# Delta rule and expert router: chunks of 32 tokens for four sequences at once, in place of chunks of 64 for two

## The chip, the cores and the metric

The kernel runs on one core of a Trainium2 chip. A core has TensorE (matrix products, results into PSUM), VectorE, ScalarE and GpSimd for everything else, SyncE as the queue that issues most DMA transfers, and 16 DMA engines behind it. PSUM has eight banks of 512 fp32 values in each of its 128 partitions. The metric is the device time of one execution in microseconds (us). Before the change it is 802.09 us, the median of three runs (800.87 to 803.17). The profile is of one execution of its own, whose span is 794.5 us.

## The reference: what is computed

Two blocks, one after the other. The first is attention by the delta rule, for 4 sequences (B) of 8 heads, 768 tokens and head size 48. Each head carries a 48x48 state from token to token:

```python
k_n = k / (np.linalg.norm(k, axis=-1, keepdims=True) + 1e-06)
for t in range(S):
    kt, vt, bt = (k_n[:, :, t], v[:, :, t], beta[:, :, t, None])
    y[:, :, t] = np.einsum('bhd,bhde->bhe', q[:, :, t], state)
    v_old = np.einsum('bhde,bhd->bhe', state, kt)
    state = state + bt[:, :, :, None] * np.einsum('bhd,bhe->bhde', kt, vt - v_old)
```

The second takes the 3072 tokens of 384 values each, finds for every token the best of 8 experts by cosine similarity, and runs the token through that expert alone:

```python
logits = xn @ en.T / tau
expert_idx = np.argmax(logits, axis=1)
...
h = np.maximum(x[mask] @ w1[e], 0.0)          # 384 -> 1024
out[mask] = gate_w[mask, None] * (h @ w2[e])  # 1024 -> 384
```

Token after token the recurrence would have 768 steps. The kernel takes it in chunks: inside a chunk the tokens depend on one another through a triangular matrix that is made of products of k with k. Its inverse is built, the chunk's values are multiplied by it ("solve"), and only then is the state brought forward, once for the chunk.

## The kernel before

A unit of work is one chunk of 64 tokens, 8 heads, and two of the four sequences, one in partitions 0 to 63 and one in 64 to 127. There are 12 chunks and two units for each, 24 units. The two units of a chunk do not depend on one another, and each depends on the unit of the same sequences one chunk earlier.

The inverse is built only of the two diagonal 32x32 blocks of each 64x64 matrix, by doubling: blocks of 2, 4, 8, 16 and 32. Each of the four levels has two steps on TensorE, `level` and `grow`. All of these steps use one helper, which issues 16 matmuls on the 64x64 tiles of the array at upper left and lower right:

```python
def apply(lhsT, rhs, times=1):
    n = rhs.shape[2]
    p = bank([128, times, H, n])
    for h in range(H):
        for i in range(2):
            mm(p[HALF[i], :, h], lhsT[HALF[i], h], rhs[HALF[i], h].unsqueeze(1).broadcast_to([C, times, n]))
    return p if times > 1 else p[:, 0]

def level(U, s):
    p = apply(U["G32"], U["T"], 2)
    yield
    U["P"] = PP[s][U["n"] % 2]
    nc.vector.copy_predicated(...)          # P <- where the mask of this level says so, p

def grow(U):
    p = apply(U["P"], U["W"], 2)[:, 0]
    yield
    U["W"] = wk.tile([128, H, BL], F32, name="W", ...)
    act_copy(U["W"], p)
    yield
    transposed_blocks(U, p)                 # T, by VectorE, out of the same bank
```

A `yield` ends a part: the parts of many units are issued in turn. In the names of the profile, `bank<-T,G` is a level's step, `bank<-W,P` a grow's, `bank<-R,WL` a solve with the inverse, `bank<-Z,G` a product with a part of the gram, `bank<-S_bd,KT` the products of k and q with the state, and `pair<-Z,KK` the update of the state.

As the inverse is known for blocks of 32 only and the chunk has 64 tokens, the chunk is solved in three steps: the first block, its influence on the second, and the whole:

```python
def of_states(U):
    V, c = U["R"], U["c"]
    if c > 0:
        p = [of_state(U, a) for a in range(2)]       # k and q times the state, a bank each
        yield
    U["R"] = narrow("R", 3)
    if c > 0:
        nc.vector.tensor_tensor(U["R"], p[0], V, op=ALU.subtract)
        yield
        U["Yq"] = narrow("Yq", 3)
        act_copy(U["Yq"], p[1])
    ...

def solve1(U):
    p = apply(U["W"], U["R"])
    yield
    U["Z1"] = narrow("Z1")
    act_copy(U["Z1"], p, K["first"])

def solve2(U):
    p = apply(U["G"][:, 0].rearrange("p j jj c -> p (j jj) c"), U["Z1"])
    yield
    nc.vector.scalar_tensor_tensor(out=U["R"], in0=p, scalar=K["second"], in1=U["R"], op0=ALU.mult, op1=ALU.add)

def solve3(U):
    p = apply(U["W"], U["R"])
    yield
    U["Z"] = narrow("Z", 3)
    act_copy(U["Z"], p)

def state(U):
    ...
    p = pair([NP, D])
    for j in range(NP):
        for i in range(2):
            for jj in range(2):
                mm(p[HALF[jj], i, j], U["K"][HALF[i], 2 * j + jj], U["Z"][HALF[i], 2 * j + jj])
    yield
    S_ = S_u[U["u"]]
    nc.vector.tensor_tensor(S_, p.rearrange("p i j d -> p j i d"), S_, op=ALU.add)
    yield
    nc.gpsimd.tensor_tensor(S_bd[U["u"]]..., S_..., K["own"]..., op=ALU.mult)   # each head on its own block
```

`first` and `second` are columns of ones and zeros that keep one half of each 64 partitions. `state` and `gram` write into a pair of banks and use all four 64x64 tiles of the array; `outputs` is one more `apply`, with the masked product of k and q.

PSUM is divided for good into four single banks and two pairs. The order in which parts are issued comes out of a small model in the kernel's own Python code, with a length for each part, that runs while the program is built. Loads are issued by SyncE, two transfers (one for a sequence) for each of k, q and v of a unit:

```python
def load(U, dst, src):
    t0 = U["c"] * C
    for i in range(2):
        nc.sync.dma_start(out=dst[i * C:(i + 1) * C],
                          in_=src[2 * U["u"] + i, :, t0:t0 + C, :].rearrange("h p d -> p h d"))
```

k and q of the first unit are loaded once ahead of everything and then once more by the unit's own `load`, whose copy is the one used. When a group of four units is through, its tokens are routed: logits, the best expert, a place in that expert's list, and the rows of x go to memory. After all groups, the second part gathers 128 tokens of one expert at a time.

Of the kernel before, what the change touches and what calls it, by code (L numbers as in the profile page):

```python
# [16 lines left out]
C = 64  # L17
BL = 32
T = 128
LEVELS = (2, 4, 8, 16)  # L20
# [3 lines left out]
def kernel(  # L24
# [35 lines left out]

    nc = tc.nc
    B, H, S, D = q.shape
    NC, NP, Dm, N = S // C, H // 2, H * D, B * S
    NU = B // 2
# [21 lines left out]

    def bank(shape):
        return ps.tile(shape, F32, name="bank", tag="bank", bufs=4)

    def pair(shape):  # L90

        t = ps.tile([128, 2, 512], F32, name="pair", tag="pair", bufs=2)
        n = 1
        for d in shape:
            n *= d
        t = t[:, :, 0:n]
        if len(shape) == 2:
            return t.rearrange("p r (a b) -> p r a b", a=shape[0])
        return t.rearrange("p r (a b c) -> p r a b c", a=shape[0], b=shape[1])
# [7 lines left out]
    hc = [128, H, C]  # L107
    jc = [128, NP, 2, C]

# [5 lines left out]
    def clear(t):  # L115
        nc.gpsimd.memset(t[:, :, D:C], 0.0)

    def load(U, dst, src):

        t0 = U["c"] * C  # L120
        for i in range(2):
            nc.sync.dma_start(out=dst[i * C:(i + 1) * C],  # L122
                              in_=src[2 * U["u"] + i, :, t0:t0 + C, :].rearrange("h p d -> p h d"))
# [11 lines left out]
    UNITS = [dict(n=n, c=n // NU, u=n % NU) for n in range(NC * NU)]  # L135
# [3 lines left out]
    bt = ac.tile([NU * H, NC, 2, C], F32, name="bt")  # L139
    for u in range(NU):  # L140
        for i in range(2):
            (nc.sync if u else nc.scalar).dma_start(out=bt[u * H:(u + 1) * H, :, i],
                                                    in_=beta[2 * u + i].rearrange("h (c t) -> h c t", t=C))
# [4 lines left out]
    half = cpool.tile([128, NU, H], F32, name="half")  # L148
    nc.vector.memset(half, 0.5)
    root = ac.tile([128, 1], F32, name="root")  # L150
    nc.scalar.activation(root, half[:, 0, 0:1], ACT.Sqrt)


    prow = ac.tile([128, C], I32, name="prow")
    nc.gpsimd.iota(prow, pattern=[[0, C]], base=0, channel_multiplier=1)
    xor_i = ac.tile([128, C], I32, name="xor_i")
    nc.gpsimd.iota(xor_i, pattern=[[1, C]], base=0, channel_multiplier=0)
    clear(KK[0])
    clear(QQ[0])
    trow = ac.tile([128, C], I32, name="trow")  # L160
    nc.vector.tensor_single_scalar(trow, prow, C - 1, op=ALU.bitwise_and)
    col_f = ac.tile([128, C], F32, name="col_f")
    nc.vector.tensor_copy(col_f, xor_i)
    nc.vector.tensor_tensor(xor_i, xor_i, trow, op=ALU.bitwise_xor)
    xor_f = ac.tile([128, C], F32, name="xor_f")
    nc.vector.tensor_copy(xor_f, xor_i)
    trow_f = ac.tile([128, C], F32, name="trow_f")
# [3 lines left out]
    id64 = ac.tile([128, 1, C], F32, name="id64")  # L171
    nc.vector.tensor_single_scalar(id64[:, 0, :], xor_f, 0.0, op=ALU.is_equal)
    id32 = ac.tile([128, 1, BL], F32, name="id32")
    nc.vector.tensor_tensor(id32[:, 0], id64[:, 0, 0:BL], id64[:, 0, BL:C], op=ALU.add)
    upper = ac.tile([128, 1, C], F32, name="upper")
    nc.vector.tensor_tensor(upper[:, 0, :], col_f, trow_f, op=ALU.is_gt)
    lower = ac.tile([128, 1, C], F32, name="lower")

    def mask(name, tri, lo, hi):
        m = ac.tile([128, 1, C], F32, name=name)  # L180
        nc.vector.scalar_tensor_tensor(out=m, in0=xor_f.unsqueeze(1), scalar=float(lo), in1=tri,
                                       op0=ALU.is_ge, op1=ALU.mult)
        nc.vector.scalar_tensor_tensor(out=m, in0=xor_f.unsqueeze(1), scalar=float(hi), in1=m,
                                       op0=ALU.is_lt, op1=ALU.mult)
        return m.bitcast(I32)
# [5 lines left out]
    W2 = [ac.tile([128, H, BL], F32, name=f"W2_{i}") for i in range(2)]  # L191
# [6 lines left out]
    betaT, sqb, quot = (ac.tile([128, NC, NU * H], F32, name=name) for name in ("betaT", "sqb", "quot"))  # L198
# [10 lines left out]
    def root_of(U):  # L209
        return sqb[:, U["c"], U["u"] * H:(U["u"] + 1) * H]  # L210

    def beta_by_token():
        psB = bank([128, NC, NU * H])
        for c in range(NC):
            nc.tensor.transpose(psB[:, c], bt[:, c].rearrange("p i t -> p (i t)"), ident[0:NU * H, 0:NU * H])
        nc.vector.tensor_copy(betaT, psB)
# [4 lines left out]
    def more_masks():  # L221
        for name, value in (("second", ALU.is_ge), ("first", ALU.is_lt)):

            K[name] = ac.tile([128, 1], F32, name=name)
            nc.vector.tensor_single_scalar(K[name], trow_f[:, 0:1], float(BL), op=value)
# [5 lines left out]
        for t in S_u:  # L231
            nc.vector.memset(t, 0.0)

    def all_masks():
        for lv in LEVELS[1:]:
            below[lv] = mask(f"below{lv}", lower, lv, 2 * lv)
        for t in XC:
            nc.gpsimd.memset(t[:, :, :, Dm:], 0.0)

        own = K["own"] = ac.tile([128, 1, 2, 1], F32, name="own")  # L240
        nc.vector.tensor_single_scalar(own[:, 0, 1], prow_p, float(C), op=ALU.is_ge)
        nc.vector.tensor_single_scalar(own[:, 0, 0], prow_p, float(C), op=ALU.is_lt)

    prow_p = ac.tile([128, 1], F32, name="prow_p")
    nc.vector.tensor_copy(prow_p, prow[:, 0:1])
    XC = [ac.tile([128, 2, NU, ROW], F32, name=f"XC{i}") for i in range(2)]
    S_u = [ac.tile([128, NP, 2, D], F32, name=f"S{u}") for u in range(NU)]
    S_bd = [ac.tile([128, NP, 2, 2, D], F32, name=f"S_bd{u}") for u in range(NU)]
# [25 lines left out]
    def late_constants3():  # L274

        prow_f = ac.tile([128, 1], F32, name="prow_f")
        nc.vector.tensor_copy(prow_f, prow[:, 0:1])
        nc.vector.tensor_single_scalar(prow_f, prow_f, float(C), op=ALU.is_ge)
        nc.vector.scalar_tensor_tensor(out=prow_f, in0=prow_f, scalar=float(S), in1=trow_f[:, 0:1],
                                       op0=ALU.mult, op1=ALU.add)  # L280
        tok_i = ac.tile([128, NC, NU], I32, name="tok_i")
        nc.gpsimd.iota(tok_i, pattern=[[C, NC], [2 * S, NU]], base=0, channel_multiplier=0)
        tok_f = ac.tile([128, NC, NU], F32, name="tok_f")
        nc.vector.tensor_copy(tok_f, tok_i)
        nc.vector.tensor_scalar(tok_f, tok_f, prow_f, None, op0=ALU.add)
        K["tokid"] = ac.tile([128, NC, NU, ID], I32, name="tokid")
        nc.vector.tensor_copy(K["tokid"], tok_f.unsqueeze(3).broadcast_to([128, NC, NU, ID]))
# [27 lines left out]
    def embeddings1():  # L315
        nc.scalar.activation(esq, emb, ACT.Square, accum_out=ess)
        nc.gpsimd.tensor_tensor(out=ess, in0=ess, in1=half[0:E, 0, 0:1], op=ALU.pow)
# [13 lines left out]
    HALF = (slice(0, C), slice(C, 2 * C))  # L331
# [11 lines left out]
    def prep2(U):  # L343
# [3 lines left out]
        nc.gpsimd.tensor_tensor(out=U["rn"], in0=U["rn"], in1=half[:, 0], op=ALU.pow)  # L347
# [15 lines left out]
    def transposes(U):  # L363
        U["KT"] = wk.tile([128, NP, 2, 128], F32, name="KT", tag="KT", bufs=4)
# [6 lines left out]
        for a in range(2):  # L371
            yield
            act_copy(U["KT"][:, :, a], ps_[a])
# [4 lines left out]
    def gram(U):  # L378

        KT = U["KT"]  # L380
        U["psG"] = p = pair([NP, 2, C])
        for j in range(NP):
            for jj in range(2):
                pr = slice(jj * C, jj * C + D)
                for i in range(2):
                    mm(p[HALF[i], jj, j], KT[pr, j, 0, HALF[i]], KT[pr, j, :, HALF[i]])
        yield
        U["G32"] = wk.tile(hc, F32, name="G32", tag="G32", bufs=3)
        for b, name in enumerate(("first", "second")):
            cols = slice(b * BL, (b + 1) * BL)  # L390
            act_copy(by_head(U["G32"])[:, :, :, cols].rearrange("p j jj c -> p jj j c"), p[:, :, :, 0, cols], K[name])
        yield
        U["W"] = W2[U["n"] % 2]
        for b in range(2):
            cols = slice(b * BL, (b + 1) * BL)
            nc.vector.copy_predicated(by_head(U["W"]).rearrange("p j jj c -> p jj j c"),  # L396
                                      up2[:, :, cols].unsqueeze(1).broadcast_to([128, 2, NP, BL]), p[:, :, :, 0, cols])
# [3 lines left out]
    def gram2(U):  # L401
        p = U["psG"]
        U["G"] = G = wk.tile([128, 2, NP, 2, C], F32, name="G", tag="G", bufs=5)
        for a in range(2):
            act_copy(G[:, a].rearrange("p j jj c -> p jj j c"), p[:, :, :, a])
            yield
        M = U["M"] = G[:, 1].rearrange("p j jj c -> p (j jj) c")
        nc.gpsimd.tensor_tensor(M, M, upper.broadcast_to(hc), op=ALU.mult)

    def transposed_blocks(U, src):  # L410
        U["T"] = wk.tile([128, H, BL], F32, name="T", tag=f"T{U['n'] % 3}", bufs=1)
        nc.vector.transpose(U["T"].rearrange("p h c -> p (h c)"), src.rearrange("p h c -> p (h c)"))  # L412

    def apply(lhsT, rhs, times=1):
# [5 lines left out]
        for h in range(H):  # L420
            for i in range(2):
                mm(p[HALF[i], :, h], lhsT[HALF[i], h], rhs[HALF[i], h].unsqueeze(1).broadcast_to([C, times, n]))
        return p if times > 1 else p[:, 0]

    def level(U, s):
# [4 lines left out]
                                  below[s].rearrange("p o (b c) -> p o b c", b=2).broadcast_to([128, H, 2, BL]),  # L430
                                  p.rearrange("p b h c -> p h b c"))

    def grow(U):
        p = apply(U["P"], U["W"], 2)[:, 0]
        yield
        U["W"] = wk.tile([128, H, BL], F32, name="W", tag=f"W{U['n'] % 3}", bufs=1)
# [4 lines left out]
    def grow_last(U):  # L441
# [3 lines left out]
        for b, name in enumerate(("first", "second")):  # L445
            act_copy(U["W"][:, :, b * BL:(b + 1) * BL], p, K[name])
# [4 lines left out]
    def of_state(U, a):  # L451

        p = bank([128, H, D])
        for j in range(NP):
            for i in range(2):
                mm(p[HALF[i], 2 * j:2 * j + 2], U["KT"][:, j, a, HALF[i]], S_bd[U["u"]][:, j, i])
        return p

    def of_states(U):

        V, c = U["R"], U["c"]
        if c > 0:
            p = [of_state(U, a) for a in range(2)]
            yield
        U["R"] = narrow("R", 3)
        if c > 0:
            nc.vector.tensor_tensor(U["R"], p[0], V, op=ALU.subtract)
            yield
            U["Yq"] = narrow("Yq", 3)
            act_copy(U["Yq"], p[1])  # L470
        else:
            nc.vector.tensor_scalar_mul(U["R"], V, -1.0)

    def solve1(U):
        p = apply(U["W"], U["R"])
        yield
        U["Z1"] = narrow("Z1")
        act_copy(U["Z1"], p, K["first"])

    def solve2(U):  # L480
# [529 lines left out]
```

## Time and profile before

| | from 0 to about 462 us: attention | from 474 us to the end: experts |
|---|---|---|
| what runs | 24 units, 7 groups of routing | 28 tiles of 128 tokens |
| TensorE busy, 160 to 220 us and 480 to 600 us | 59.6 of 60 us | 120.0 of 120 us |
| VectorE busy, same stretches | 34.7 of 60 us | 12.9 of 120 us |
| ScalarE busy | 25.8 of 60 us | 13.1 of 120 us |
| GpSimd busy | 26.2 of 60 us | 23.1 of 120 us |
| share of the DMA engines' time | 0.20 | 0.98 |

Between the two, TensorE stands for 12.6 us until the first gathered tokens arrive.

How such a page is read. A row of the groups has the source line, the engine, the operation, what is written and read by the program's names, the shape and the count; then after the first bar the busy time of the group and the mean of one instruction, and after the second the idle time of that engine just before them with what ended most of it. In order of time, a line has the start, the length, the engine, the line, the operation and the count of a run of like instructions. Matmuls overlap one another: a matmul's own length is far more than its share of TensorE's time, which is the distance from start to start. The line of 40 slices gives the busy share of each fortieth of the span in tenths. Most matmuls stem from one helper line (L334), so they are told apart by their tiles. One matmul statement in fp32 shows as two records.

### The profile page before, as it was taken

The numbers are of one execution on the slowest core, as the hardware profiler recorded it, in microseconds if no ns is written. First come the engines' busy times: TensorE is split into PE (matmuls) and PEld (weight loads), VectorE is DVE, ScalarE is ACT, GpSimd is POOL, SyncE is SP. The second block draws the span as 40 slices with busy tenths as digits, with TensorE's granted clock in tenths as the row PEclk, the third lists the DMA queues.
The fourth block names the chain that finished last, engine by engine and source line by source line (L and its number), as shares of the span: only waits on it lengthen the run. The fifth ranks groups of instructions, "written<-read, shape, count | busy, mean of one in ns | idle before, by whom it ended". The sixth has DMA issues, their size and how long they took to land.

```text
span 794.5 us, 30513 instructions
## 1 busy us (share of the span) xinstructions
PE 725.1 (91%) x13770; PEld 651.1 (82%) x13770; DVE 284.2 (36%) x696; ACT 219.9 (28%) x485; POOL 254.3 (32%) x277
## 2 busy tenths in 40 slices
PE   2889899899989989998998829999999999999993
PEld 2789899799989989998998828877788877788872
DVE  5756546366454636654553330011011011011010
ACT  2544343535344433434352201110111010111010
POOL 4843333365164435525423121221122221122220
PEclk9999999999999999999999759999999999999997
DMA  6653421313132231202001129999999999999996
GB/s 120 121 142 85 130 43 24 86 24 63 20 75 44 39 85 25 44 4 56 5 3 42 28 63 390 390 366 326 343 318 320 330 317 331 347 311 333 318 317 240
DMA packets 137446, 132.46 MB, mean 167 GB/s; under 512 B 86266, under 2 KB 121505, under 8 KB 137314
## 3 DMA queue, kind: packets, MB, share of 16 engines
q1 hardware_dynamic: 132562, 119.15, 48.6%
q0 software_dynamic: 4544, 11.27, 3.8%
q8 instruction: 110, 1.80, 0.9%
q14 instruction: 22, 0.18, 0.1%
q10 hardware_dynamic: 208, 0.05, 0.0%
HBM read 118.78 MB, written 12.45 MB: 165 GB/s over the span
## 4 chain that ended last, share of the span: by engine, by line
PE 61%; DMA 17%; issue 10%; DVE 6%; POOL 2%; ACT 1%; SPq 1%; another core or an unknown queue 0%; POOLq 0%; ACTq 0%; DVEq 0%
PE bank L334 37%; DMA out_dram<-y,ids 14%; PE acc L895 8%; PE acc L902 8%; PE pair L334 3%; PE bank L369 2%; DMA ids<-idmap 1%; PE bank L530 1%; DVE T L412 1%; DVE W L396 1%; DVE P L429 1%; DMA k_in<-in_k_dram 1%; DVE rn L352 1%; PE acc L886 1%; SPq L122 1%
## 5 line engine op out<-in xcount | busy, mean ns | idle before, releaser
L334 PE MATMUL bank<-T,G 64*64 64x64 f32 x3072 | 110.8, 224 | 7.1 <-issue 3.2
L334 PEld LDWEIGHTS bank<-T,G 64*64 64x64 f32 x3072 | 102.1, 139 | 11.1 <-issue 5.0
L897 ACT ACTIVATE hT<-acc 128x512 f32<-128x512 f32 x56 | 33.5, 597 | 280.4 <-PE acc L895 272.8
L334 PE MATMUL bank<-W,P 64*64 64x64 f32 x3072 | 105.5, 220 | 5.1 <-DVE P L429 3.7
L334 PEld LDWEIGHTS bank<-W,P 64*64 64x64 f32 x3072 | 98.1, 136 | 6.4 <-issue 3.6
L895 PEld LDWEIGHTS acc<-xTm,w 128*128 128x128 f32 x864 | 99.3, 192 | 4.8
L905 POOL DMA_INDIRECT out_dram<-y,ids x28 | 28.5, 1017 | 229.2 <-DVE y L904 212.1
L895 PE MATMUL acc<-xTm,w 128*128 128x128 f32 x864 | 99.4, 275 | 0.0
L902 PE MATMUL acc<-w,hT 128*128 128x384 f32 x288 | 95.9, 486 | 0.0
L429 DVE COPY_PREDICATED P<-below,bank 128x512 f32<-128x512 int32 x96 | 69.8, 731 | 44.4 <-PE bank L334 39.2
L902 PEld LDWEIGHTS acc<-w,hT 128*128 128x128 f32 x288 | 53.3, 190 | 33.4
L887 DVE COPY xTm<-acc 128x384 f32<-128x384 f32 x29 | 16.2, 558 | 152.4 <-PE acc L886 152.4
L334 PE MATMUL bank<-R,WL 64*64 64x48 f32 x1536 | 58.4, 221 | 9.5 <-issue 9.5
L503 POOL TENSOR_TENSOR S_bd<-S,own 128x768 f32<-128x768 f32 x22 | 32.3, 1466 | 99.4 <-DVE S L501 99.4
L904 DVE TENSOR_SCALAR y<-acc,xg 128x384 f32<-128x384 f32 x28 | 17.3, 618 | 128.9 <-PE acc L902 128.9
L334 PEld LDWEIGHTS bank<-R,WL 64*64 64x64 f32 x1536 | 53.3, 138 | 11.7 <-issue 11.7
L895 PEld LDWEIGHTS acc<-xTm,w_first 128*128 128x128 f32 x480 | 57.3, 198 | 3.5 <-DVE xTm L887 1.1
L895 PE MATMUL acc<-xTm,w_first 128*128 128x128 f32 x480 | 57.5, 282 | 0.7 <-DVE xTm L887 0.7
L334 PE MATMUL bank<-Z,G 64*64 64x48 f32 x1536 | 55.1, 220 | 2.3 <-issue 1.8
L334 PEld LDWEIGHTS bank<-Z,G 64*64 64x64 f32 x1536 | 51.4, 138 | 2.7 <-issue 1.9
L902 PE MATMUL acc<-w_first,hT 128*128 128x384 f32 x160 | 53.3, 486 | 0.0
L347 POOL TENSOR_TENSOR rn<-rn,half 128x8 f32<-128x8 f32 x24 | 39.5, 1647 | 34.2 <-DVE rn L345 31.7
(167 smaller groups left out, 901.3 us busy)
## 6 DMA issues: line engine op xcount, KB each, us to landing
w<-in_moe_w_dram SPq DMA_DIRECT2D x40, 1536.0 KB
w_first<-in_moe_w_dram SPq DMA_DIRECT2D x20, 1536.0 KB
k_in<-in_k_dram SPq DMA_DIRECT2D x50, 96.0 KB
QQ<-in_q_dram SPq DMA_DIRECT2D x50, 96.0 KB
x_dram<-XC SPq DMA_DIRECT2D x24, 200.0 KB
v_in<-in_v_dram SPq DMA_DIRECT2D x48, 96.0 KB
idmap<-none SPq DMA_DIRECT2D x1, 1792.0 KB
w_first<-in_moe_w_dram SPq DMA_DIRECT2D x8, 192.0 KB
```

The lines of the kernel that those rows point to most:

```text
L122: nc.sync.dma_start(out=dst[i * C:(i + 1) * C], in_=src[2 * U["u"] + i, :, t0:t0 + C, :].rearrange("h p d -> p h d"))
L334: nc.tensor.matmul(out_, lhsT=lhsT, rhs=rhs, start=start, stop=True, skip_group_check=True)
L347: nc.gpsimd.tensor_tensor(out=U["rn"], in0=U["rn"], in1=half[:, 0], op=ALU.pow)
L369: nc.tensor.transpose(p[:, j], src[:, 2 * j:2 * j + 2, :].rearrange("p h d -> p (h d)"), ident)
L429: nc.vector.copy_predicated(U["P"].rearrange("p h (b c) -> p h b c", b=2), below[s].rearrange("p o (b c) -> p o b c", b=2).broadcast_to([1 ...
L503: nc.gpsimd.tensor_tensor(S_bd[U["u"]].rearrange("p j i jj d -> p (j i) jj d"), S_.rearrange("p j i d -> p (j i) d").unsqueeze(2).broadcas ...
L887: nc.vector.tensor_copy(t.xT, psX)
L895: nc.tensor.matmul(psH[:, i, :], lhsT=t.w1[:, j, (f + i) * 128:(f + i + 1) * 128], rhs=t.xT[:, j, :], start=(j == 0), stop=(j == KC - 1))
L897: nc.scalar.activation(t.hT[:, f:f + 4, :], psH, ACT.Relu)
L902: nc.tensor.matmul(psO, lhsT=t.hT[:, f, :], rhs=t.w2[:, f, :], start=(f == 0), stop=(f == NF - 1))
L904: nc.vector.tensor_scalar_mul(y, psO, t.x[:, Dm:Dm + 1])
L905: nc.gpsimd.indirect_dma_start(out=out[:, :], out_offset=bass.IndirectOffsetOnAxis(ap=t.ids[:, 0:1], axis=0), in_=y, in_offset=None, bound ...
```

## The change

The chunk becomes as long as the blocks of the inverse. A unit is now 32 tokens of all four sequences: two sequences share each half of the partitions, 32 partitions each. There are 24 chunks and one unit for each, so again 24 units of the same size, but each unit depends on the one just before it. Since the inverse covers the whole chunk, it is applied directly, in one step in place of three. The state of two sequences has to be told apart inside one half: the right side of the state's update is widened to two copies of Z, each with the other sequence's tokens set to zero, and the products with the state are computed for both and cleared by `first` and `second`. The state is now kept in its block form only, so GpSimd's spreading goes away.

PSUM's eight banks are kept in one list. A part takes one or two of them and hands each back as soon as its last reader is issued. The order of all parts is written down in a table, a number for each part and each unit, and the parts are sorted by it.

The diff, cut to its core:

```diff
-C = 64
-BL = 32
+C = 32
+PC = 2 * C
...
     def bank(shape):
-        return ps.tile(shape, F32, name="bank", tag="bank", bufs=4)
+        b = free.pop(0)
+        taken.append([b])
+        t = psum[b // 2][:, b % 2, 0:512]
...
     def load(U, dst, src):
-        t0 = U["c"] * C
-        for i in range(2):
+        t0 = U["n"] * C
+        for i in range(B):
...
     def transposes(U):
-        U["KT"] = wk.tile([128, NP, 2, 128], F32, name="KT", tag="KT", bufs=4)
+        U["KT"] = wk.tile([128, NP, 2, 4, C], F32, name="KT", tag="KT", bufs=4)
+        U["kT"] = wk.tile([128, NP, 2, PC], F32, name="kT", tag="kT")
...
+            if p is ps_[0]:
+                yield
+                act_copy(U["kT"].rearrange("d j p c -> d j (p c)"), p)
...
+            ps_ = [bank([128, H, D]) for o in range(2)]
+            for j in range(NP):
+                for o in range(2):
+                    for i in range(2):
+                        mm(ps_[o][HALF[i], 2 * j:2 * j + 2], U["KT"][:, j, i, 2 * o:2 * o + 2], S_bd[:, i, j, o])
...
+        nc.vector.scalar_tensor_tensor(out=U["R"], in0=ps_[1], scalar=K["second"], in1=V, op0=ALU.mult,
+                                       op1=ALU.subtract)
+        nc.vector.scalar_tensor_tensor(out=U["R"], in0=ps_[0], scalar=K["first"], in1=U["R"], op0=ALU.mult,
+                                       op1=ALU.add)
+        yield
+        parts = [narrow("Yq1"), narrow("Yq2")]
+        act_copy(parts[0], ps_[0], K["second"])
+        act_copy(parts[1], ps_[1], K["first"])
+        yield
+        U["Yq"] = narrow("Yq", 3)
+        nc.gpsimd.tensor_tensor(U["Yq"], parts[0], parts[1], op=ALU.add)
+
+    def solve(U):
         p = apply(U["W"], U["R"])
         yield
-        U["Z1"] = narrow("Z1")
-        act_copy(U["Z1"], p, K["first"])
-
-    def solve2(U):
-        p = apply(U["G"][:, 0].rearrange("p j jj c -> p (j jj) c"), U["Z1"])
-        yield
-        nc.vector.scalar_tensor_tensor(out=U["R"], in0=p, scalar=K["second"], in1=U["R"], op0=ALU.mult, op1=ALU.add)
-
-    def solve3(U):
-        p = apply(U["W"], U["R"])
+        U["Zx"] = wk.tile([128, H, 2, D], F32, name="Zx", tag="Zx")
+        act_copy(U["Zx"][:, :, 0], p, K["first"])
+        yield
+        nc.vector.tensor_scalar(U["Zx"][:, :, 1], p, K["second"], None, op0=ALU.mult)
         yield
         U["Z"] = narrow("Z", 3)
         act_copy(U["Z"], p)
...
-                    mm(p[HALF[jj], i, j], U["K"][HALF[i], 2 * j + jj], U["Z"][HALF[i], 2 * j + jj])
+                    mm(p[HALF[jj], i, 2 * j:2 * j + 2], U["K"][HALF[i], 2 * j + jj], U["Zx"][HALF[i], 2 * j + jj])
         yield
-        S_ = S_u[U["u"]]
-        nc.vector.tensor_tensor(S_, p.rearrange("p i j d -> p j i d"), S_, op=ALU.add)
-        yield
-        nc.gpsimd.tensor_tensor(S_bd[U["u"]]...
+        for jj in range(2):
+            own = S_bd[HALF[jj], :, :, :, jj].rearrange("p i j o d -> p i (j o) d")
+            nc.vector.tensor_tensor(own, p[HALF[jj]], own, op=ALU.add)
...
+    KEYS = {
+        "load": (-11464,), "prep1": (-8895,), "prep2": (-7076, -7075), "prep3": (-5816, -5815), "scale_v": (-5757,),
+        "transposes": (-3773, -3772, -3771, -3770), "gram": (-2683, -2682, -2681, -2680), "gram2": (92, 93, 3874),
...
+        "of_states": (7169, 7170, 7171, 7172), "solve": (8244, 8245, 8246, 8247), "state": (9397, 9398),
...
+    BASE = (-6100, -2180, 1870, 5807, 9591, 13404, 17210, 20989, 24801, 28644, 32590, 36251, 40157, 44051, 47913,
+            51716, 55405, 59261, 62974, 66795, 70813, 74479, 78270, 82247)
...
+    parts = [(BASE[U["n"]] + key, i, U["n"], name, part) for i, (U, name, part, key) in enumerate(
+        (U, name, part, key) for U in UNITS for name in KEYS for part, key in enumerate(KEYS[name]))]
```

## What was predicted

> **What bounds the kernel now.** I read the page first (busy shares, the 40 slices, the costliest groups), then the engines' busy time in chosen stretches, then TensorE in order of time inside one steady stretch, then the issue queue of SyncE at the start.
>
> ```profile
> PE 725.1 (91%) x13770; PEld 651.1 (82%) x13770; DVE 284.2 (36%) x696; ACT 219.9 (28%) x485; POOL 254.3 (32%) x277
> ...
> PE   2889899899989989998998829999999999999993
> ...
> DVE  5756546366454636654553330011011011011010
> ...
> L334 PE MATMUL bank<-R,WL 64*64 64x48 f32 x1536 | 58.4, 221 | 9.5 <-issue 9.5
> ...
> L334 PE MATMUL bank<-Z,G 64*64 64x48 f32 x1536 | 55.1, 220 | 2.3 <-issue 1.8
> ```
>
> The dip in slices 23 and 24 divides the program: about 462 us of attention, a gap, then from 474 us the expert stage, which the change leaves alone. In both TensorE is at eight or nine tenths; VectorE, its nearest follower, is at half in attention. One matmul statement leaves two records: 16 statements x 24 units x 2 stages give 768, and the row of R,WL shows 1536. That row is solve1 and solve3, the row of Z,G is solve2 and the outputs. A record's mean of 220 ns is no cost: matmuls overlap. The cost is from start to next start, which TensorE in order of time gives:
>
> ```profile
> 186.35 1.10 PE L334 MATMUL pair<-KT 48*64 48x128 f32 x32
> ...
> 303.28 1.11 PE L334 MATMUL bank<-R,WL 64*64 64x48 f32 x32
> 304.20 1.98 PE L334 MATMUL bank<-T,G 64*64 64x64 f32 x61
> 305.97 0.26 PE L334 MATMUL pair<-Z,KK 64*64 64x48 f32 x2
> 306.00 0.28 PE L334 MATMUL bank<-T,G 64*64 64x64 f32 x3
> 306.07 0.66 PE L334 MATMUL pair<-Z,KK 64*64 64x48 f32 x30
> 306.54 1.14 PE L334 MATMUL bank<-W,P 64*64 64x64 f32 x32
> 307.48 1.11 PE L334 MATMUL bank<-Z,G 64*64 64x48 f32 x32
> ```
>
> A solve step of 48 columns takes 304.20 - 303.28 = 0.92 us; Z,G takes 0.92 us as well (the next group starts at 308.40). A level step of 64 columns takes 0.94 us (306.54 to 307.48). The state update takes 0.57 us (305.97 to 306.54), the gram with 128 columns 0.92 us (the next group starts at 187.27). So a step that runs dense on TensorE is worth about 0.92 us whatever its width up to 64, and attention is a string of such steps. The stretches say the same:
>
> ```profile
> core 0: us, PE busy (x) PEld busy (x) DVE busy (x) ACT busy (x) POOL busy (x), PEclk, DMA share, GB/s
> 154.66:295.70 141.04, 135.47 (x3993) 131.71 (x3994) 76.73 (x182) 59.41 (x138) 64.30 (x64) 0.99 0.24 50
> 0.00:100.00 100.00, 74.60 (x2108) 70.93 (x2110) 60.54 (x156) 40.77 (x90) 49.19 (x69) 1.00 0.52 119
> 430.00:474.00 44.00, 25.47 (x437) 23.45 (x436) 15.38 (x74) 6.81 (x18) 11.79 (x17) 0.68 0.19 47
> ```
>
> Eight units take 141.04 us: 17.6 us a unit, 16.9 of them with TensorE busy, VectorE 9.6, ScalarE 7.4, GpSimd 8.0. The start loses 25 us of TensorE, the drain before 474 us loses 18.5.
>
> **What the Trainium skill says.** "TensorEngine Tiling (Array Packing)", section Performance Considerations (Instruction Overhead), gives each matmul a fixed floor, so that few columns cost as much as some sixty. The trace agrees: 48 and 64 columns differ by 0.02 us a step. Removing whole steps pays, narrowing them would not. The same page, Tiling Modes (Key Properties), says that tiles of the array run independently. The state update and the gram use all four 64x64 tiles and cost 0.57 us at 48 and 0.92 us at 128 columns; the solves use only the two diagonal ones and cost 0.92 us at 48. "PSUM — Partial Sum Buffer", section PSUM bank collisions raise a hardware error, says two engines must not touch the same bank and partitions at once, reads included. The groups of instructions before agree: VectorE's transposes out of a bank stood idle 42.3 us in all for ScalarE's copy W, which reads the same bank. The new solve has three readers of one bank, so they go one after the other. "VectorE: DVE Perf Modes", section Why PSUM operands drop a tier, says fp32 from PSUM runs at the basic rate; the add into S at 384 elements took 540 ns here.
>
> **The change part by part.**
>
> Removed from TensorE per unit: solve1 and solve2, 2 x 0.92 = 1.84 us. With it go one ScalarE copy of 581 ns and one VectorE operation of 613 ns, both beside other work.
>
> Added to TensorE: the state update now has 96 columns. Between 0.57 us at 48 and 0.92 us at 128 a straight line gives 0.57 + 0.35 x 48/80 = 0.78 us: +0.21. Gram, levels, growth, outputs, of_states keep their count and width. Net per unit -1.63 us; over 24 units -39 us. As all sequences are in one unit, only unit 0 lacks of_states and only the last lacks the state update; before, two units lacked each: +1.4 (2.86 us for two steps of of_states) and +0.8, about +2 us.
>
> VectorE per unit: of_states has two operations in place of one (+0.6), Zx one (+0.5), the state add two half-partition operations of 768 elements in place of one of 384. By the 540 ns row and an element rate estimated from it and the page, one is about 0.95 us, so +1.4; solve2's 0.6 goes. 9.6 becomes about 11.5 us. ScalarE: a third copy for the transposes (+0.6) and a second for Yq (+0.5) give 8.5. GpSimd: S_bd of 1.47 us goes, the sum of Yq of 0.83 comes. All stay under 16 us a unit.
>
> The recurrent chain is now passed 24 times, not 12 times for two independent halves. Its latency from state to state: of_states 1.4, two VectorE operations 1.2, solve 0.92, ScalarE 0.6, VectorE 0.5, state 0.8, two adds 1.9, about 0.1 for each of six hand-overs: 8 us. That is half a unit's 16 us. In the order of the changed kernel, four steps of TensorE (3.3 us) stand between state and of_states, against 2.1 us needed, and three to five between of_states and solve, and solve and outputs. So the chain should lie beside other work. The tightest place is ScalarE after of_states, where Yq, three copies for the transposes and two for M precede the W that the next level needs: I count 0.2 to 0.4 us of wait in a unit there.
>
> Gaps: TensorE's occupied time a unit before is 16.9 of 17.6 us. The table places parts per unit evenly instead of in pairs, and loads come unit by unit instead of in bursts, so I expect 0.4 us of gap in place of 0.7: -0.3 x 20 = -6 us.
>
> Start: SyncE's queue decides.
>
> ```profile
> 0.82 1.43 SPq L122 DMA_DIRECT2D k_in<-in_k_dram  x2
> 2.29 1.31 SPq L122 DMA_DIRECT2D QQ<-in_q_dram  x2
> 3.64 1.57 SPq L142 DMA_DIRECT2D bt<-in_beta_dram  x2
> 5.25 1.33 SPq L122 DMA_DIRECT2D k_in<-in_k_dram  x2
> ```
>
> Each issue holds the queue some 0.65 us, the small bt as long as the large k_in. Each load is now four transfers in place of two. The first unit's k that is really used is the second load (the first is issued ahead of the loop, then again by the unit), whose issue ended at 6.6 us and becomes the 13th to 16th: 0.82 + 16 x 0.68 = 11.7. The first gram at 16.4 us goes to about 21, and the next unit's transposes from 21.9 to 26. The levels' latency hides none of that: +4.5 us.
>
> Drain: the last two units were independent halves of one chunk; now the last waits for the state of the one before. After that update come two adds, of_states, R and a solve in place of two solves and a correction: +2.5 us.
>
> Sum: -39 + 2 - 6 + 4.5 + 2.5 = -36. From 220 to 400 us the granted clock was 0.97 and after 430 us 0.68, so the removed steps were a little dearer than at full clock: -3. In all -39: 802 - 39 = 763 us.
>
> **Rivals.** (1) The recurrence becomes the bound: if an in-order queue delays one link by more than the 1 us of slack, every unit pays. At +2 us a unit the gain is gone, 800 us. Against it: 8 us of latency in 16. For it: VectorE would be over 70% busy, and both its halves of the state add stand behind a level's copy of 0.73 us. (2) The loads or their issue bind: 12 issues of 0.65 us a unit are 7.8 us of 16, so no bound in steady state, but a start of +10 us is possible, 770. (3) The table is better than I think and also closes the gaps of the start, where TensorE is busy 74.6 of 100 us: -10 to -15, about 750. (4) VectorE and ScalarE limit by reading one bank in turn: 1 us a unit, 787.
>
> **Range and chances.** The removed work is sure to within a few us, as TensorE is dense. Uncertain are the gaps (0 to 1 us a unit, -16 to +8), the start (0 to +10) and the drain (0 to +5). From these I take 744 to 784. The threshold of 2% lies at 786, beyond the range: faster 0.91, within 2% 0.07, slower 0.02.
>
> **What would show it.** Right: the row of R,WL falls to 768 records and that of Z,G splits off half; a unit takes 15.5 to 16 us in the steady stretch; the state update's step takes about 0.8 us; first gram near 21 us; the expert stage still takes 320 us. Wrong: TensorE in the steady stretch waits on VectorE's S_bd or R, or on ScalarE's W, for over 1 us a unit; a unit stays at 17 us or more; the first gram comes later than 27 us.

## The result and the profile after

The changed kernel takes 921.1 us (917.2 to 923.4); the kernel before took 802.0 us beside it. The ratio is 1.148 (95% interval 1.144 to 1.152). The prediction was 763 us, range 744 to 784: wrong in direction, by 158 us.

The page of the changed kernel: busy shares, slices, and the groups that answer to those shown of before (count, busy time and mean of one after the first bar and the count, idle time of TensorE just before them after the second).

```profile
PE 742.5 (81%) x12298; PEld 648.7 (70%) x12298; DVE 330.9 (36%) x742; ACT 233.4 (25%) x533; POOL 245.2 (27%) x278
...
PE   2776787877678778778776777489999999999994
...
DVE  4444555555445565545542345401111111111110
...
L350 PE MATMUL psum<-W,P 64*64 64x64 f32 x3072 | 124.2, 240 | 61.4 <-DVE P L453 43.9
...
L350 PE MATMUL psum<-T,G 64*64 64x64 f32 x3072 | 119.4, 233 | 27.4 <-DVE T L436 15.8
...
L350 PE MATMUL psum<-R,WL 64*64 64x48 f32 x768 | 30.7, 236 | 22.2 <-DVE T L436 16.4
```

For comparison, the row of W,P before, with 5.1 us of idle time in place of 61.4:

```profile
L334 PE MATMUL bank<-W,P 64*64 64x64 f32 x3072 | 105.5, 220 | 5.1 <-DVE P L429 3.7
```

The removed work is gone: R,WL has 768 records in place of 1536, and TensorE has 1472 fewer in all. But TensorE, at nine tenths in attention before, is at seven or eight. The dip now lies in slice 26: the expert stage begins at 602.1 us, before at 474.1. It lasts 320 us in both, so all of the loss is ahead of it, in attention. No engine took TensorE's place; VectorE is at half, as before. The stretches say so too (columns as in the prediction):

```profile
core 0: us, PE busy (x) PEld busy (x) DVE busy (x) ACT busy (x) POOL busy (x), PEclk, DMA share, GB/s
0.00:100.00 100.00, 58.61 (x1088) 53.73 (x1088) 46.26 (x117) 30.23 (x68) 30.60 (x53) 0.85 0.29 62
200.00:300.00 100.00, 77.29 (x1952) 71.29 (x1954) 50.01 (x105) 37.00 (x89) 35.38 (x37) 0.91 0.29 66
```

From state update to state update a unit takes 22.2 us on the mean, (572.56 - 106.44) / 21; before it was 17.6. So one asks what TensorE waits for. The view of waits of the changed kernel (total us, times, longest):

```profile
PE psum L350 <- DVE P L453: 53.0, 47, 2.9
PE psum L350 <- DVE T L436: 35.2, 22, 4.2
...
PE psum L350 <- ACT Z L398: 9.6, 5, 2.7
PE psum L350 <- ACT KT L398: 6.4, 5, 2.1
```

P and T are operands of levels and grows, so this could be plain lateness. It is not that alone, as the view of one product shows: all matmuls that read WL, with what ended TensorE's idle time before them.

```profile
L350 PE MATMUL psum<-R,WL x768: 205/218/340, 64.8 to 579.8; 64*64 64x48 f32 x192
its engine sat idle before it (us, times) until:
  DVE T L436: 16.4, 10
```

The solve reads R and WL. It doesn't read T at all, and yet waited ten times for VectorE to have made T. One such case in order of time, TensorE, VectorE and ScalarE in turn:

```profile
200.90 1.10 PE L350 MATMUL psum<-W,P 64*64 64x64 f32 x32
203.45 1.14 PE L350 MATMUL psum<-R,WL 64*64 64x48 f32 x32 [1.45 <-issue]
```

```profile
198.66 0.62 DVE L492 SCALAR_TENSOR_TENSOR R<-psum,first,R 128x384 f32<-128x384 f32 x1
...
202.94 0.45 DVE L436 STREAM_TRANSPOSE T<-psum 128x256 f32<-128x256 f32 x1 [1.09 <-ACT W L398]
```

```profile
197.33 0.47 ACT L398 ACTIVATE WL<-psum,second 128x256 f32<-128x256 f32 x1
...
202.48 0.43 ACT L398 ACTIVATE W<-psum 128x256 f32<-128x256 f32 x1
```

R was ready at 199.28 (198.66 + 0.62) and WL at 197.80. The solve started at 203.45, 0.06 us after T was done (203.39). The view puts this one wait down to "issue"; in the program as built this solve waits for the instruction that makes this T. What T has to do with it: T reads the result of the grow step at 200.90, which lies in one half of a two-bank PSUM tile, and the solve writes into the other half of the same tile. The changed kernel gives banks out singly but declares them as four tiles of two banks, `psum[b // 2][:, b % 2]`. In the program as built, TensorE's matmuls carry 337 waits on VectorE or ScalarE, each with the number of the instruction that it waits for: 169 are for an instruction that touches neither an operand nor the bank, only the other half of the tile, 160 are for an operand, 8 for the bank itself. Of the 24 solves, 22 wait for an instruction on the other half, 12 of these for one that makes T. In the kernel before, none is of the first kind: 365 are for an operand and 108 for the last user of the buffer that is taken anew.

**Theory H1:** a wait is kept per PSUM tile, so products into one half wait for the readers of the other. **Rival theories:** H2, the order in the table makes T, P and W late (W at 202.48 stood behind seven other ScalarE copies); H3, the latency of 24 recurrent steps in place of 12 bounds the kernel.

### The profile page after: what moved, and what is told of

It reads as the page before. It is cut to its first block, busy times and chain, and to the rows that moved or that the text cites. A ratio compares the mean times of both kernels' runs of the same rounds, so it can differ in the third digit from the quotient of the medians.

```text
span 921.7 us, 27906 instructions
## 1 busy us (share of the span) xinstructions
PE 742.5 (81%) x12298; PEld 648.7 (70%) x12298; DVE 330.9 (36%) x742; ACT 233.4 (25%) x533; POOL 245.2 (27%) x278
## 3 DMA queue, kind: packets, MB, share of 16 engines
q1 hardware_dynamic: 135202, 119.16, 42.3%
## 4 chain that ended last, share of the span: by engine, by line
PE 24%; DMA 20%; issue 11%; DVE 11%; ACT 5%; POOL 0%; POOLq 0%; DVEq 0%; SPq 0%; ACTq 0%
DMA out_dram<-y,ids 19%; PE psum L350 17%; DVE S_bd L525 3%; PE acc L807 3%; DVE P L453 2%; PE acc L814 2%; DVE T L436 1%; ACT Yq L398 1%; PE psum L549 1%; DVE W L418 1%; ACT KT L398 1%; DVE XC L539 1%; DVE R L490 1%; PE psum L387 1%; ACT G L398 1%
## 5 line engine op out<-in xcount | busy, mean ns | idle before, releaser
L350 PE MATMUL psum<-W,P 64*64 64x64 f32 x3072 | 124.2, 240 | 61.4 <-DVE P L453 43.9
L350 PEld LDWEIGHTS psum<-W,P 64*64 64x64 f32 x3072 | 113.4, 153 | 70.0 <-DVE P L453 49.6
L350 PE MATMUL psum<-T,G 64*64 64x64 f32 x3072 | 119.4, 233 | 27.4 <-DVE T L436 15.8
L350 PEld LDWEIGHTS psum<-T,G 64*64 64x64 f32 x3072 | 108.9, 147 | 34.8 <-DVE T L436 14.9
L453 DVE COPY_PREDICATED P<-below,psum 128x512 f32<-128x512 int32 x96 | 69.0, 718 | 57.0 <-PE psum L350 55.1
L398 ACT ACTIVATE W<-psum 128x256 f32<-128x256 f32 x72 | 28.0, 390 | 141.6 <-PE psum L350 139.7
L500 POOL TENSOR_TENSOR Yq<-Yq,Yq 128x384 f32<-128x384 f32 x23 | 23.0, 1000 | 149.1 <-ACT Yq L398 128.0
L373 POOL TENSOR_TENSOR KK<-k_in,rn 128x384 f32<-128x384 f32 x24 | 20.0, 832 | 158.4 <-DVE rn L370 150.1
L363 POOL TENSOR_TENSOR rn<-rn,half 128x8 f32<-128x8 f32 x24 | 39.7, 1655 | 73.9 <-DVE rn L361 73.9
L436 DVE STREAM_TRANSPOSE T<-psum 128x256 f32<-128x256 f32 x72 | 32.3, 449 | 63.1 <-ACT W L398 62.2
L350 PE MATMUL psum<-R,WL 64*64 64x48 f32 x768 | 30.7, 236 | 22.2 <-DVE T L436 16.4
```

The lines of the kernel that those rows point to most:

```text
L350: nc.tensor.matmul(out_, lhsT=lhsT, rhs=rhs, start=start, stop=True, skip_group_check=True)
L363: nc.gpsimd.tensor_tensor(out=U["rn"], in0=U["rn"], in1=half, op=ALU.pow)
L373: nc.gpsimd.tensor_tensor(U["K"][:, :, 0:D], U["k"], rn.unsqueeze(2).broadcast_to([128, H, D]), op=ALU.mult)
L398: nc.scalar.activation(out_, in_, ACT.Copy, scale=scale)
L453: nc.vector.copy_predicated(U["P"].rearrange("p h (b c) -> p h b c", b=2), below[s].rearrange("p o (b c) -> p o b c", b=2).broadcast_to([1 ...
L500: nc.gpsimd.tensor_tensor(U["Yq"], parts[0], parts[1], op=ALU.add)
```

## Experiments

Chips differ: the kernel before takes about 803 us on some that were used here and 780 us on others. Each ratio is therefore to the kernel before on the same chip.

**Own tiles: the grouping undone, all else kept.** Four one-bank tiles and two two-bank tiles, as before; the order of instructions on the four compute engines is that of the changed kernel (SyncE issues the same transfers, some of them in another order).

```diff
-    psum = [ps.tile([128, 2, 512], F32, name=f"psum{i}") for i in range(4)]
+    psum = [ps.tile([128, 2, 512], F32, name=f"psum{i}") for i in range(2)]
+    psum1 = [ps.tile([128, 512], F32, name=f"single{i}") for i in range(4)]
...
-        b = free.pop(0)
+        b = next(b for b in free if b < 4)
+        free.remove(b)
         taken.append([b])
-        t = psum[b // 2][:, b % 2, 0:512]
+        t = psum1[b]
```

> The changed kernel with one thing undone: the eight PSUM banks are declared as before, four tiles of one bank and two tiles of two banks, and steps that need one bank take only the former; the order of all instructions and every instruction stay. Theory H1 (waits are kept per PSUM tile, so a product into one half of a two-bank tile waits for the readers of the other half): the false waits go, 755 to 790 us, and TensorE's waits for VectorE's P and T, 88 us in the changed kernel, come to under 20 us. H2 (the table's order puts W behind other ScalarE copies and T and P behind the state's additions): nothing but the bank changes, so 890 us or more. H3 (the latency of the 24 recurrent steps bounds the kernel): 890 us or more.

Measured: 803.6 us, ratio 1.0007 (0.999 to 1.0025). H2 and H3 are out as the main cause: with the same order and the same recurrence, 117 us are gone. But the range expected of H1 is missed on the high side, by 14 us, and TensorE's waits for P and T came down from 88 to 24 us, not to under 20; some 40 us to the predicted 763 remain.

**Another choice of bank, the two-bank tiles kept.**

```diff
-        b = free.pop(0)
+        b = min(free, key=lambda b: (b ^ 1 not in free, max(free.index(x) for x in (b, b ^ 1) if x in free)))
+        free.remove(b)
```

> The changed kernel with its four two-bank tiles kept, and only the choice among the free banks changed: a bank whose other half is free too goes first, and of those the one whose halves have been unused longest. H1: the products still share tiles, but mostly with a step further back, whose readers are further on: 790 to 880 us. H2 and H3: the choice of bank is no matter, 905 to 935 us.

Measured: 844.8 us, ratio 1.051 (1.046 to 1.057), as H1 has it. The program has more waits of the kind in question, 189 in place of 169, and loses less. So their number is no measure of the loss.

**One part of the change alone, in the kernel before.** Its four single banks become the halves of two tiles.

```diff
     def bank(shape):
-        return ps.tile(shape, F32, name="bank", tag="bank", bufs=4)
+        given.append(1)
+        i = (len(given) - 1) % 4
+        t, n = halves[i // 2][:, i % 2, 0:512], 1
```

> The kernel before with one part of the change alone: its four one-bank buffers become the halves of two two-bank tiles, taken in the same turn; nothing else. H1: about a third as many waits for a reader of the other half arise as in the changed kernel; at the changed kernel's mean price (its excess over the prediction, some 150 us, over its 169 such waits, 0.9 us each) that is some 55 us: 830 to 880 us. H2 and H3: the grouping of the banks is no matter, 795 to 812 us.

Measured: 881.7 us, ratio 1.098 (1.090 to 1.105). The grouping alone, with none of the new algorithm or table, slows the kernel before by a tenth, a little more than the 880 us expected at most.

Its control, with the same fixed turn of four buffers, each a tile of its own (`t, n = fixed[(len(given) - 1) % 4], 1`):

> The control of the run of the kernel before with halves: the same four buffers in the same fixed turn, but each a tile of its own. H1: within 1% of the kernel before, since what slowed that run by 10% is that two buffers share a tile. If the fixed turn in place of the pool's was the cause, it is slower by 5% or more as well.

Measured: 803.1 us, ratio 1.0002 (0.998 to 1.002). The fixed turn costs nothing; sharing a tile does. In the two programs as built every product goes into the same bank of the eight, so a conflict of neighbouring banks in the hardware is no rival either: it would slow both.

**The recurrence cut.** The products with the state read zeros, so no unit waits for the one before:

```diff
-                        mm(ps_[o][HALF[i], 2 * j:2 * j + 2], U["KT"][:, j, i, 2 * o:2 * o + 2], S_bd[:, i, j, o])
+                        mm(ps_[o][HALF[i], 2 * j:2 * j + 2], U["KT"][:, j, i, 2 * o:2 * o + 2], S_0)
```

> The changed kernel with the recurrence cut: the products with the state read a constant tile of zeros in its place, so that no unit waits for the state of the one before (the state is still formed and added up, but not read: what is computed is attention within each chunk alone). H3 (recurrent latency): 800 us or less, TensorE no longer waits. H1 and H2: 895 to 925 us, since the recurrence is not what TensorE waits for.

Measured: 927.4 us, ratio 1.154 (1.149 to 1.159), 2 us above the range expected: no gain at all. H3 falls.

**What remains in the own tiles.** Their waits of TensorE between 100 and 400 us (total us, times, longest) are led by the transposes of a later unit's k and q (L389), which waited for ScalarE's Yq copies to free a bank:

```profile
PE single L389 <- ACT Yq L400: 12.1, 13, 1.5
PE single L352 <- DVE P L455: 8.4, 17, 1.6
PE single L352 <- DVE T L438: 6.6, 13, 1.4
```

This is a true wait for a bank: four singles go round, where the change meant eight. So a version with six one-bank tiles and one of two for gram; the state's product goes into two singles.

```diff
-    psum = [ps.tile([128, 2, 512], F32, name=f"psum{i}") for i in range(4)]
+    psum = ps.tile([128, 2, 512], F32, name="pair0")
+    psum1 = [ps.tile([128, 512], F32, name=f"single{i}") for i in range(6)]
...
-        p = pair([NP * 2, D])
+        ps_ = [bank([128, NP * 2, D]) for i in range(2)]
...
         for jj in range(2):
-            own = S_bd[HALF[jj], :, :, :, jj].rearrange("p i j o d -> p i (j o) d")
-            nc.vector.tensor_tensor(own, p[HALF[jj]], own, op=ALU.add)
+            for i in range(2):
+                own = S_bd[HALF[jj], i, :, :, jj].rearrange("p j o d -> p (j o) d")
+                nc.vector.tensor_tensor(own, ps_[i][HALF[jj]], own, op=ALU.add)
```

> The changed kernel with six tiles of one bank and one tile of two: only gram takes the two-bank tile, and the state's product goes into two one-bank tiles, so that its two additions become four of half the size (some 0.3 us more of VectorE a unit); the rest and the order stay. H1 with its remainder in the bank count (the run with own tiles, 803.6 us, still has 27 us of TensorE waits between 100 and 400 us, 12 of them of transposes for ScalarE's Yq copies, whose banks come free late because four singles go round): most of these waits go, 765 to 790 us. If the remaining waits are of the table's order (a product placed too close behind its own operand) the two more banks change little: 797 to 808 us.

Measured: 765.2 us, but on the faster chip, where the kernel before takes 780 us: ratio 0.982 (0.978 to 0.986). To part the chip from the banks, both versions ran once more on one chip, with the kernel before:

> The kernel before, unchanged, for a profile from the same chip as the next two (its time was 802 us beside the run with own tiles and 780 us beside the run with six singles). If the chip is the cause, its granted clock differs and its waits do not: a clock near 0.97 where the time is near 780 us, near 0.955 where it is near 802 us.

> The changed kernel with own tiles once more, on one chip with the six singles: equal to the kernel before within 1%, as it was (ratio 1.0007), if the number of free banks is what parts it from the six singles; 0.98 to 0.985 if the chip alone was the difference.

> The changed kernel with six one-bank tiles once more, on one chip with the own tiles: 0.965 to 0.985 of the kernel before, and 2% or more under the own tiles, if two more banks to go round take away the waits for ScalarE's Yq copies; equal to the own tiles within 0.5% if the chip was the difference.

Measured: the kernel before 803.1 us at a granted clock of 0.956; own tiles 804.1 us, ratio 1.0008 (0.999 to 1.003); six singles 768.6 us, ratio 0.957 (0.952 to 0.962). Two more banks are worth 35 us, the chip is not the cause, and this version beats both kernels (the ratio is a little under the 0.965 expected at least). Its page, and its waits of TensorE between 100 and 400 us:

```profile
PE 695.7 (91%) x12298; PEld 614.5 (80%) x12298; DVE 331.5 (43%) x788; ACT 229.9 (30%) x533; POOL 245.1 (32%) x278
...
PE   1687999999999999999999469999999999999993
...
L352 PE MATMUL single<-T,G 64*64 64x64 f32 x3072 | 113.9, 225 | 12.1 <-DVE T L438 8.7
...
L352 PE MATMUL single<-W,P 64*64 64x64 f32 x3072 | 110.5, 222 | 5.8 <-DVE P L455 4.0
```

```profile
PE single L352 <- issue: 4.8, 8, 1.8
PE single L352 <- DVE T L438: 4.1, 6, 1.8
```

TensorE is at nine tenths all through attention with the very order of steps that had it at seven or eight. Idle time ahead of W,P fell from 61.4 to 5.8 us.

**A dose of the cause, put back.** Of the six singles, two become halves of one tile:

```diff
+    halves = ps.tile([128, 2, 512], F32, name="halves")
-    psum1 = [ps.tile([128, 512], F32, name=f"single{i}") for i in range(6)]
+    psum1 = [halves[:, 0], halves[:, 1]] + [ps.tile([128, 512], F32, name=f"single{i}") for i in range(4)]
```

> The six singles with a measured dose of the cause put back: two of the six one-bank buffers become the halves of one tile, the other four stay tiles of their own; order and instructions stay. H1: some 67 waits on the reader of the other half come back; at 0.7 us each (117 us over the changed kernel's 169, from the run with own tiles) some 47 us on 768 us: 795 to 835 us. If sharing mattered only where most banks share: 765 to 780 us.

Measured: 865.9 us, ratio 1.109 (1.103 to 1.115), where the six singles had 0.982 on a chip on which the kernel before took the same 780 us. The direction is H1's, but the size was missed: 100 us, not 47. The waits of TensorE in this run, whole program:

```profile
PE halves L353 <- DVE P L456: 27.3, 19, 2.4
PE halves L353 <- DVE T L439: 19.8, 13, 2.6
...
PE halves L353 <- ACT KT L401: 10.4, 5, 3.0
...
PE halves L353 <- ACT Z L401: 6.9, 2, 4.9
PE halves L353 <- DVE S_bd L529: 6.5, 2, 4.1
```

These five come to 71 us in 41 waits; even spread over all 67 that came back it is over 1 us each, not the 0.7 assumed. Most of the rest lies in TensorE's busy time, 720.0 us against 691.4 in the six singles, for the same instructions. Every product goes into the same bank here as in the six singles, so this pair too leaves no room for a conflict of banks. A price per wait from one kernel doesn't carry to another.

**The recurrence cut in the six singles**, to see whether it has become the bound now:

> The six singles with the recurrence cut: the products with the state read constant zeros (what is computed is attention within each chunk alone; the state is still formed). If the recurrence had slack, as the prediction had it (8 us of latency in a unit of 16): 760 to 770 us. If it has become the bound once the waits for the other half are gone: 745 us or less.

Measured: 761.0 us, ratio 0.975 (0.969 to 0.981) against 0.982: some 4 us at most, as the two intervals overlap. The recurrence has slack.

## Why the prediction was wrong

The step that failed is "Gaps": "0.4 us of gap in place of 0.7: -0.3 x 20 = -6 us". In its place the changed kernel had 4.9 us of gap a unit: between 100 and 400 us TensorE stood idle for 65.7 us, at 22.2 us a unit. In the six singles it stood for 9.7 us there, 0.5 us a unit, so the table and the loads alone do give what was predicted. PSUM was not in the sum: neither that banks are declared in twos nor how many of them a product can take without a wait. Both stood in the diff and in the kernel. With the instructions and their order unchanged, undoing the grouping gave 117 us back, and two more independent buffers another 35; the two together are the 158 us of error but for 6.

How the loss is made up, from changed kernel to own tiles, spans 921.7 and 801.8 us: TensorE's idle time falls from 179.2 to 97.0 us (82), and its busy time for the same instructions from 742.5 to 704.8 us (38). A part of the second term goes with the granted clock, 0.924 and 0.960; an estimate from these two alone is 704.8 x (0.960 / 0.924 - 1), some 27 us. The Trainium skill, "Perfetto Trace Analysis", section Matmul Optimizations, says that the matmul engine scales power with utilization, so that batches should run back to back. The traces agree as far as they go: one record of W,P took 240 ns on the mean in the changed kernel, with TensorE busy for 81% of the span, and 220 in the own tiles, with 88%. That waiting is paid for twice, in idle time and in the clock, fits this, but no run here changes the one without the other.

Point by point, with the six singles as the version in which the other steps can be seen:

- **TensorE's removed and added steps: right.** There R,WL at 170.62 is followed at 171.54, 0.92 us, and the state update at 161.36 at 162.14, 0.78 us, the predicted figure. Units without routing take 14.8 to 15.7 us, and the mean with routing is 16.0 (predicted 15.5 to 16).
- **VectorE: right in size and harmless, as said.** 284.2 to 330.9 us is 1.9 us a unit, as predicted; an addition into the state took 951 ns (estimated 0.95 us). **ScalarE** grew by 0.6 us a unit, about half of what was predicted.
- **"The tightest place"**, W behind the other ScalarE copies, is where the chain of the case above began, but by itself it costs little: in the six singles the same queue order leaves TensorE 0.5 us of waits a unit (8.9 us in 300). Only the shared tile hands W's lateness on, through T, to a solve that needs neither.
- **Start: right in sum, in part by luck.** In the first 100 us TensorE was busy for 69.5 us in the six singles and 73.9 in the kernel before on that chip: 4.4 us, predicted 4.5. But the first gram ran at 20.01 us (predicted 21) and the next unit's transposes at 26.59 (predicted 26), one early and one late. The four halved transfers of the unit's own k held the queue for 1.93 us, 0.48 us each and not 0.68, and the last was issued by 10.66 us (8.73 + 1.93), not by 11.7; in the changed kernel:

```profile
8.73 1.93 SPq L138 DMA_DIRECT2D k_in<-in_k_dram  x4
```

- **Drain: not seen.** In the last 53 us before the first gathered tokens are used TensorE stood idle for 18.7 us in the six singles and for 18.8 in the kernel before on that chip; predicted were 2.5 us more.
- **Rivals.** The recurrence (1) is refuted by both runs that cut it. The loads (2) bind at the start alone, where TensorE's first wait, for bt, grew from 7.0 to 10.2 us. The table (3) did not close the gaps of the start. Reading one bank in turn (4) is a link of the chain: VectorE's T stood 62.2 us for ScalarE's W in the changed kernel, 42.3 before. But it is no bound of its own, as it stood 38.1 us in the six singles. Of the signs of being wrong, "a unit stays at 17 us or more" came true, but the waits that were named, on S_bd, R or W, did not: TensorE waited most on P and T.

In all, the six singles came to 0.957 of the kernel before on one chip, 35 us of the predicted 39, and to 0.982 on the other, 15 us; predicted was 763 / 802 = 0.951. So the estimate of the algorithm nearly held on the kind of chip that it was made for. The estimate of the changed kernel did not, since it never asked what else a product waits for before it may write into PSUM.

What stays open: why two shared banks cost nearly as much as eight. That what counts is how late the other half's reader is, and not how many such waits there are, would fit the runs with 62, 67, 169 and 189 of them (79, 100, 117 and 41 us over the same kernel with own or more tiles) but was not measured wait by wait. Gram's and the state's evacuation split over eight one-bank tiles was not tried.

## What to carry to other kernels

A buffer is as large as the tile that the program keeps waits for, not as the bank that holds it: before counting on n independent banks, count tiles, and look in the waits for a releaser that is no operand of the instruction released. The Trainium skill, "Perfetto Trace Analysis", section Matmuls, has independent groups rotate through different PSUM banks so that evacuation overlaps the next products; the runs here agree where each rotating bank is a tile of its own (768.6 us), and not where two share a tile (921.1 us, with the same order of products). When a diff hands buffers out anew, price that line like any other.

## What was not expected of the hardware

Among the versions of the changed kernel the mean granted clock goes with TensorE's busy share of the span: 0.924 at 81%, 0.937 at 83% (two halves), 0.960 at 88% (own tiles) and 0.964 at 91% (six singles). In the changed kernel no single wait of TensorE in attention was longer than 4.2 us after the first 20 us, so even short ones go with a lower clock here. It is no rule: on one and the same chip the kernel before had 0.956 at 91% and the own tiles 0.958 at 88%, and the first 100 us of the kernel before, with TensorE busy for 74.6 us, ran at 1.00, while the changed kernel had 0.91 from 200 to 300 us, busy for 77.3. What sets the clock is not shown by these runs. And one kernel differs between chips by more than another: the kernel before took 803.5 and 779.8 us on two chips, the six singles 768.6 and 765.2 us on the same two. The clocks go the same way for the kernel before (0.956 and 0.971 on the mean of its runs) and hardly differ for the six singles (0.966 and 0.965), but no run here explains why one kernel is granted less on one chip and the other is not.
